# Adaptive-norm attention and gated feed-forward: the loop's products on tiles of 64 rows and 32 columns

## Chip, cores and metric

One core of a Trainium2 chip runs the whole program. The metric is the device time of one execution in microseconds (us). A program's engines are called PE (TensorE), DVE (VectorE), ACT (ScalarE), POOL (GpSimd) and SP (SyncE, which issues the DMAs); PEld is PE's weight load.

## The reference, cut to what matters

The input x has 2048 rows of 512. There are 32 query heads of 16, which share one key and one value head, and a feed-forward of 1792.

```
mod = silu(c) @ w_mod                      # six rows: sa, ca, ga, sb, cb, gb
h = layernorm(x) * (1 + ca) + sa
q, k, v = h @ wq, h @ wk, h @ wv           # q: 32 heads of 16; k, v: one head of 16
p = softmax(q k^T / 4)                     # 32 x 2048 x 2048
x = x + ga * ((p @ v) @ wo)
h = layernorm(x) * (1 + cb) + sb
x = x + gb * ((sigmoid(h @ w_gate) * (h @ w_up)) @ w_down)
```

## The kernel before, in words

A prologue normalises x, transposes it, and makes keys, values and the first q products. Then comes a loop of 512 steps: 32 units (4 blocks of 512 query rows, 8 units of four heads in each) with 16 steps, one for each 128 keys. A tail finishes the last block. Products other than the values are in 2-byte numbers, split into high and low halves and added up as three products; P, V and the transposes are 4-byte.

One step (the body from line 928) does the following on PE, in this order, which the code writes out and `Ordered` (line 110) pins:

- `scores(n)` four times (line 938): `st_tile` (495) multiplies 64 rows of keys and queries into a bank `st` of 128 keys by 512 queries, which ACT turns into P by an exponential; `a_tile` (443) multiplies queries and keys of a later unit (19 steps ahead) into a bank `sa`, of which DVE takes the row maximum `mx`. Both work on one half of the array's rows, and always on opposite halves, so the two run side by side. There are two `st` banks and two `sa` banks.
- `values()` twice with work in it (line 948): `pv` (509) multiplies P of two steps ago with V into the banks `c` and `c1`. One call is eight 4-byte matmuls on tiles of 64 rows and 32 columns, two row halves by four heads, with 256 queries each. In the trace each of them appears as two matmuls: a burst is 16, two passes of eight.
- `piece()` four times (line 908): a piece of what else PE has to do for an earlier block. These products come as a `Couple` (143) of two groups, one on each row half with its own bank: output projection `po`, gate and up projections `pgu`, down projection `pd`. One n of a couple is one such pair of 64-row products. There are two banks for them, so a couple starts when both banks of the last have been read by ACT and DVE (or ACT alone).
- in the first block `light` (915) instead: one or two pairs of q products a step, 24 in 17 steps.

The loop's feed-forward work begins with the second block. `plan` (885) takes a couple of 24 or more pairs, gives it n steps by `RATE` (4.5 pairs a step), and `places` (862) says how many pairs go into each of the steps' four places: the first half of the pairs is dealt over 2n - 1 places, then two places stay empty, and the second half is dealt over 2n - 1 more. `lead` keeps count of what runs ahead.

Unit 0 differs: its `st` bank is made by four products of 128 queries, and its values come as 16 matmuls of 128 queries a call. The first 76 `sa` products are issued ahead of the loop. In unit 31 there are none left.

Of the kernel before, what the change touches and what calls it, by code (L numbers as in the profile page):

```python
# [16 lines left out]
P = 128  # L17
# [33 lines left out]
RATE = 4.5  # L51
# [15 lines left out]
def adaln_mqa_glu_kernel(  # L67
# [35 lines left out]
    def sbank(name):  # L103
        return psum["s"].tile([P, 512], F32, tag=name, name=name, bufs=SBANKS[name]) if "s" in psum else bank(name)
# [5 lines left out]
    class Ordered:  # L110
        def __init__(self, engine):
            self.engine = engine
# [5 lines left out]
    pinned = []  # L118
    pe, dve, act = Ordered(nc.tensor), Ordered(nc.vector), Ordered(nc.scalar)

    class Group:
        def __init__(self, stage, n, name, term, end, begin=None):
            self.stage, self.n, self.name, self.term, self.end, self.begin = stage, n, name, term, end, begin
# [16 lines left out]
    class Couple:  # L143
# [3 lines left out]
        def part(self, n0, n1):  # L147
            if n0 == 0:
                for g in self.gs:
                    g.open()  # L150
            m = self.n // 2
            for n in range(n0, n1):
                for j in range(2):
                    g = self.gs[j ^ (n >= m)]
                    l_, r_ = g.term(n % m, slice(64 * j, 64 * j + 64))
                    pe.matmul(g.bank, l_, r_, start=(n == 0), stop=(n == self.n - 1))
            if n1 == self.n:
                for k, g in enumerate(self.gs):
                    g.end(g.bank, k == 1)
# [162 lines left out]
    kp = cp.tile([P, S], F16, name="kp")  # L322
# [111 lines left out]
    def get_q(i):  # L434
        b, u = units[i]
        o = u // 2
        if (b, o) not in qps:
            assert (b, o) in qdone
            load_q(b, o)
        return qps[b, o], 2 * (u % 2)  # L440


    def a_tile(i, n):
        qp, pr0 = get_q(i)
        if i not in mxs:
            mxs[i] = wp.tile([P, 4, 4, 4], F32, tag="mx", name="mx", bufs=2)
        h = n % 4
        kc, qt = (n // 4 % 4, n // 16) if i == 0 else (n // 16, n // 4 % 4)
        j, pr = heads[h]
        sa = sbank("sa")  # L450
        pe.matmul(sa, qp[64 * j:64 * j + 64, pr0 + pr, qt * P:(qt + 1) * P],  # L451
                  kp[64 * j:64 * j + 64, kc * 512:(kc + 1) * 512], start=True, stop=True)
        dve.tensor_reduce(mxs[i][:, 2 * j + pr, qt, kc:kc + 1], sa, axis=AX.X, op=ALU.max)  # L453
        if i == 0 and n % 16 == 15:
            pend.append((i, n // 16, n // 16 + 1))
        elif i > 0 and n == 63:
            pend.append((i, 0, 4))
# [32 lines left out]
    def parts(i, t):  # L490
        if i == 0:
            return [(4 * (t % 4) + n, slice(n * P, (n + 1) * P), slice(t // 4 * P, (t // 4 + 1) * P)) for n in range(4)]
        return [(t, slice(0, QB), slice(0, QB))]

    def st_tile(i, t, pr, j):
        qp, pr0 = get_q(i)
        if j == 0:
            P_["p"] = P2.tile([P, 2, 512], F32, tag=f"P{pr}", name=f"P{pr}", bufs=PBUFS)
        p_ = P_["p"]
        s_ = sbank("st")  # L500
        for kb, cols, qs in parts(i, t):
            pe.matmul(s_[:, cols], kp[64 * j:64 * j + 64, kb * P:(kb + 1) * P],
                      qp[64 * j:64 * j + 64, pr0 + pr, qs], start=True, stop=True)
        act.activation(p_[:, j], s_, AF.Exp, scale=0.25)
        Ps[i, t, 2 * pr + j] = p_[:, j]

# [133 lines left out]
    class Transposes:  # L640
        stage, n = "tr", 4
# [215 lines left out]
    run = []  # L857
    lead = [0.0]
# [1 line left out]


    def places(m, n):
        k = 2 * n - 1
        half = [m * (z + 1) // k - m * z // k for z in range(k)]
        return half + [0, 0] + half

    def pick(s):
        while main and main[0][0] is None:
# [16 lines left out]
    def plan(s):  # L885
        if s < NU * NKB:
            return
        if not run:
            g = pick(s)
            if g is None:  # L890
                lead[0] = 0.0
                return
            if g.stage == "tr":
                n, sizes = 1, [0, 4, 0, 0]
            else:
                least = -(-g.n // MOST)
                n = min(max(least, round((g.n + lead[0]) / RATE)), len(units) * NKB - s)
                if n < least:
                    spare.insert(0, g)
                    return  # L900
                sizes = places(g.n // 2, n)
            at = 0
            for z in sizes:
                run.append((g, at, at + z))
                at += z
        lead[0] += sum(z[2] - z[1] for z in run[:4]) - RATE

    def piece():
        if run:
            g, n0, n1 = run.pop(0)  # L910
            if n1 > n0:
                g.part(n0, n1)
# [10 lines left out]
    for i, (b, u) in enumerate(units):  # L923
# [4 lines left out]
        for kb in range(NKB):  # L928
# [9 lines left out]
            def scores(n):  # L938
                st_tile(i, kb, n // 2, n % 2)
                if an + (n ^ 1) < len(alist):  # L940
                    a_tile(*alist[an + (n ^ 1)])
# [10 lines left out]
                        pv(*z)  # L952

            scores(0)
            piece()
            values()
            scores(1)
            if b == 0:
# [2 lines left out]
            scores(2)  # L961
            for z in rows:
                z()
            piece()
            values()
            scores(3)
            piece()
# [65 lines left out]
```

## Time and profile before

| what | us |
|---|---|
| median of 3 runs (lowest to highest) | 1969.54 (1966.88 to 1969.86) |
| the profiled execution | 1967.33 |
| its span in the trace | 1965.5 |
| PE busy | 1865.7 |
| DVE busy | 1471.8 |
| ACT busy | 1242.5 |
| POOL busy | 642.3 |

The profile's page gives for each engine its busy time and number of instructions; for groups of equal instructions the count, the busy time together, the mean of one in ns, and the idle time of the engine ahead of them with what ended it. In the trace a matmul's record starts when its data start to move and ends by a model, about 0.16 us after the next one may start; so PE is read by the distance of starts, not by busy time. `64*128` in a row is the tile of the array that is used (64 rows, 128 columns), `64x512` the moving operand. A view in order of time merges equal neighbours: start, length from the first start to the last end, and the count. A view of stretches gives each engine's busy time and count within it, the clock granted to PE, and DMA.

### The profile page before, as it was taken

To read this page: it belongs to the slowest core of one execution; us is meant where nothing else is said; L and a number is where in the kernel's file an instruction comes from. 1 tells how busy PE (TensorE), PEld (TensorE's weight loads), DVE (VectorE), ACT (ScalarE), POOL (GpSimd) and SP (SyncE) were. 2 spreads that over 40 slices of the span, in tenths; PEclk is the share of its full clock that TensorE was granted. 3 is DMA by queue.
4 is the path that set the end of the run, shared out by engine and by line. 5 is a ranking of instruction groups with operands and counts; after the bars stand their busy time and mean duration, and the time that the engine had idled before them with its cause. 6 is when DMAs were issued, how large, how long until landed. Compare 5 with 4: busy or idle time off the path is not lost.

```text
span 1965.5 us, 58671 instructions
## 1 busy us (share of the span) xinstructions
PE 1865.7 (95%) x25787; PEld 630.8 (32%) x25787; DVE 1471.8 (75%) x2407; ACT 1242.5 (63%) x2263; POOL 642.3 (33%) x744
## 2 busy tenths in 40 slices
PE   6889999999999999999999999999999999998998
PEld 3344222222223333333323333333323333322444
DVE  8889999999887777777787777777788777741411
ACT  3258778888676666666676666666667666665100
POOL 4213444454353231322254131323144132122333
PEclk9679999999999999999999999999999999998999
DMA  6102222321001110101001010111010010011211
GB/s 239 57 13 81 67 90 89 102 62 55 22 18 40 34 40 5 46 32 33 31 26 40 27 51 5 35 32 42 22 37 30 26 51 16 16 33 42 74 65 54
DMA packets 66328, 92.41 MB, mean 47 GB/s; under 512 B 14752, under 2 KB 41376, under 8 KB 66072
## 3 DMA queue, kind: packets, MB, share of 16 engines
q1 hardware_dynamic: 66072, 88.66, 14.0%
q8 instruction: 202, 3.31, 0.7%
q14 instruction: 54, 0.44, 0.1%
HBM read 67.68 MB, written 16.22 MB: 43 GB/s over the span
## 4 chain that ended last, share of the span: by engine, by line
PE 82%; DVE 6%; ACT 5%; issue 2%; DMA 2%; POOL 1%; SPq 1%; POOLq 0%; ACTq 0%; DVEq 0%
PE c L116 28%; PE st L116 19%; PE pgu L116 10%; PE sa L116 9%; PE pd L116 4%; PE pgu L139 4%; DVE mx L116 3%; PE pd L139 2%; ACT P L116 2%; PE pq L116 2%; PE po L116 1%; ACT th L116 1%; PE sa L451 1%; DVE mx L453 1%; SPq L551 1%
## 5 line engine op out<-in xcount | busy, mean ns | idle before, releaser
L116 DVE TENSOR_REDUCE mx<-sa 128x1 f32<-128x512 f32 x1972 | 1269.3, 685 | 291.3 <-PE sa L116 287.5
L116 ACT ACTIVATE P<-st 128x512 f32<-128x512 f32 x2048 | 1137.0, 595 | 494.3 <-PE sa L116 443.2
L116 PE MATMUL st<-qp,kp 64*128 64x512 f16 (+1 forms) x2240 | 748.6, 364 | 15.0 <-ACT P L116 10.6
L116 PE MATMUL sa<-kp,qp 64*128 64x512 f16 x1972 | 730.6, 381 | 7.5 <-DVE mx L116 6.8
L116 PE MATMUL c<-P,V 64*32 64x256 f32 (+1 forms) x16896 | 680.1, 382 | 0.0
L116 PEld LDWEIGHTS c<-P,V 64*32 64x32 f32 x16896 | 193.5, 105 | 425.4 <-issue 407.4
L116 PEld LDWEIGHTS <-kp 64*128 64x128 f16 x2240 | 183.3, 94 | 441.5 <-issue 424.3
L116 PE MATMUL pgu<-h2h,gw 64*128 64x512 f16 x1312 | 258.2, 377 | 26.2 <-ACT th L116 18.0
L116 PEld LDWEIGHTS <-qp 64*128 64x128 f16 x1972 | 175.5, 93 | 108.0 <-issue 32.1
L116 PE MATMUL pgu<-h2l,gw 64*128 64x512 f16 x656 | 134.9, 378 | 0.0
L116 PEld LDWEIGHTS <-gw 64*128 64x128 f16 x1968 | 100.8, 94 | 105.2 <-issue 37.0
L732 POOL TENSOR_SCALAR th<-th 128x512 f32<-128x512 f32 x41 | 25.4, 619 | 313.2 <-ACT th L116 313.0
L542 POOL TENSOR_TENSOR cs<-cs,cs 128x512 f32<-128x512 f32 x31 | 39.3, 1268 | 181.6 <-DVE cs L116 169.3
L478 POOL TENSOR_SCALAR mh<-m 16x128 f16<-16x128 f32 (+1 forms) x34 | 9.8, 289 | 264.5 <-ACT m L116 264.5
L424 POOL MEMSET qp<- 32x2048 f16 x32 | 57.6, 1799 | 55.6 <-PE sa L116 49.3
L139 PE MATMUL pgu<-h2h,gw 128*128 128x512 f16 x240 | 71.9, 379 | 0.0
L738 POOL TENSOR_TENSOR gl<-th,gh 128x512 f16<-128x512 f32 x56 | 64.8, 1158 | 4.7
L116 PE MATMUL pd<-wdh,gh 64*128 64x512 f16 x280 | 56.4, 376 | 4.9 <-ACT ot L116 2.6
L726 ACT ACTIVATE th<-pgu 128x512 f32<-128x512 f32 x15 | 9.0, 597 | 80.6 <-PE pgu L139 80.6
L735 DVE SCALAR_TENSOR_TENSOR th<-th,pgu 128x512 f32<-128x512 f32 x15 | 10.3, 685 | 65.6 <-PE pgu L139 53.3
L737 POOL TENSOR_SCALAR gh<-th 128x512 f16<-128x512 f32 x56 | 34.8, 621 | 69.1 <-DVE th L735 65.5
L116 DVE COPY u<-pgu 128x512 f32<-128x512 f32 x41 | 27.9, 680 | 37.1 <-PE pgu L116 37.0
(167 smaller groups left out, 1435.9 us busy)
## 6 DMA issues: line engine op xcount, KB each, us to landing
gw<-wD SPq DMA_DIRECT2D x56, 512.0 KB
wD<-gw SPq DMA_DIRECT2D x14, 512.0 KB
wm<-in_w_mod_dram SPq DMA_DIRECT2D x6, 1024.0 KB
qp<-qD SPq DMA_DIRECT2D x96, 64.0 KB
xall<-in_A_x_dram SPq DMA_DIRECT2D x4, 1024.0 KB
qD<-q SPq DMA_DIRECT2D x16, 256.0 KB
raw<-cs SPq DMA_DIRECT2D x128, 32.0 KB
xr<-in_A_x_dram SPq DMA_DIRECT2D x16, 256.0 KB
```

The lines of the kernel that those rows point to most:

```text
L116: return (lambda *a, **k: keep(f_(*a, **k))) if pinned else f_
L139: pe.matmul(self.bank, l_, r_, start=(n == 0), stop=(n == self.n - 1))
L424: pool.memset(qp[j:j + 32], 0.0)
L451: pe.matmul(sa, qp[64 * j:64 * j + 64, pr0 + pr, qt * P:(qt + 1) * P], kp[64 * j:64 * j + 64, kc * 512:(kc + 1) * 512], start=True, stop=True)
L453: dve.tensor_reduce(mxs[i][:, 2 * j + pr, qt, kc:kc + 1], sa, axis=AX.X, op=ALU.max)
L478: pool.tensor_scalar(mh[:, 0], m32, 1.0, 0.0, op0=ALU.mult, op1=ALU.add)
L542: pool.tensor_tensor(cs, cs, cs1, op=ALU.add)
L551: sp.dma_start(dst[DH * g:DH * (g + 1)], cs[32 * hh + r0:32 * hh + r0 + DH])
L732: pool.tensor_scalar(th, th, 1.0, 1.0, op0=ALU.add, op1=ALU.mult)
L735: dve.scalar_tensor_tensor(th, th, 1.0, p_, op0=ALU.add, op1=ALU.mult)
L737: pool.tensor_scalar(hi, th, 1.0, 0.0, op0=ALU.mult, op1=ALU.add)
L738: pool.tensor_tensor(lo, th, hi, op=ALU.subtract)
```

## The change

A helper splits a product into four over the columns of the array. It is used for the scores `st`, for `sa` inside the loop, and for the pairs of couples; the q products of `light` are couples too. Products ahead of the loop and in the tail keep their 128 columns. The values had 64x32 tiles already.

The second part is where pieces stand. `piece()` is called at two places of a step instead of four: after the second scores and after the fourth. `places` deals the first half of a couple's pairs over n - 1 places and the second half over n, with one empty place between, so that a place holds two or three pairs.

```diff
+    def columns(dst, l_, r_, start, stop):
+        for c_ in range(0, P, 32):
+            pe.matmul(dst[c_:c_ + 32], l_[:, c_:c_ + 32], r_, start=start, stop=stop)
...
-                    pe.matmul(g.bank, l_, r_, start=(n == 0), stop=(n == self.n - 1))
+                    columns(g.bank, l_, r_, n == 0, n == self.n - 1)
...
-        pe.matmul(sa, qp[64 * j:64 * j + 64, pr0 + pr, qt * P:(qt + 1) * P],
-                  kp[64 * j:64 * j + 64, kc * 512:(kc + 1) * 512], start=True, stop=True)
+        l_, r_ = qp[64 * j:64 * j + 64, pr0 + pr, qt * P:(qt + 1) * P], kp[64 * j:64 * j + 64, kc * 512:(kc + 1) * 512]
+        if pinned:
+            columns(sa, l_, r_, True, True)
+        else:
+            pe.matmul(sa, l_, r_, start=True, stop=True)
...
-            pe.matmul(s_[:, cols], kp[64 * j:64 * j + 64, kb * P:(kb + 1) * P],
-                      qp[64 * j:64 * j + 64, pr0 + pr, qs], start=True, stop=True)
+            columns(s_[:, cols], kp[64 * j:64 * j + 64, kb * P:(kb + 1) * P],
+                    qp[64 * j:64 * j + 64, pr0 + pr, qs], True, True)
...
-        k = 2 * n - 1
-        half = [m * (z + 1) // k - m * z // k for z in range(k)]
-        return half + [0, 0] + half
+        k = [n - 1, n]
+        first, second = ([m * (z + 1) // q_ - m * z // q_ for z in range(q_)] for q_ in k)
+        return first + [0] + second
...
-                n, sizes = 1, [0, 4, 0, 0]
+                n, sizes = 1, [4, 0]
...
-        lead[0] += sum(z[2] - z[1] for z in run[:4]) - RATE
+        lead[0] += sum(z[2] - z[1] for z in run[:2]) - RATE
...
             scores(0)
-            piece()
             values()
             scores(1)
...
             for z in rows:
                 z()
-            piece()
             values()
             scores(3)
             piece()
```

On PE, around a burst of values in the middle of the loop (a step of the third block), there stood these rows: the last score product of one place (`sa`, weights from the queries `qp`), the burst on the banks `c` and `c1`, and the first score product of the next place (`st`, weights from the keys `kp`).

```order
L116 LDWEIGHTS qp
L116 MATMUL sa<-kp,qp 128x512
L116 MATMUL c<-P_14015,V 32x256 x2
L116 MATMUL c<-P_14042,V 32x256 x2
L116 MATMUL c_14158<-P_14015,V 32x256 x2
L116 MATMUL c_14158<-P_14042,V 32x256 x2
L116 LDWEIGHTS kp
L116 MATMUL st<-qp,kp 128x512
```

Now the same place reads as follows; of `sa` the last of four column products is shown, of `st` the first of four.

```order
L116 LDWEIGHTS qp
L116 MATMUL sa<-kp,qp 32x512
L116 MATMUL c<-P_23979,V 32x256 x2
L116 MATMUL c<-P_24036,V 32x256 x2
L116 MATMUL c_24160<-P_23979,V 32x256 x2
L116 MATMUL c_24160<-P_24036,V 32x256 x2
L116 LDWEIGHTS kp
L116 MATMUL st<-qp,kp 32x512
```

The order is the same; every output ahead of the burst and behind it now has the burst's 32 columns.

Between the bursts stood the pieces, on PE in the same stretch of the loop: one pair of gate or up products (`pgu`, weights from `gw`) after each pair of scores.

```order
L116 LDWEIGHTS gw
L116 MATMUL pgu<-h2h,gw 128x512
L116 LDWEIGHTS gw
L116 MATMUL pgu<-h2h,gw 128x512
L116 LDWEIGHTS kp
L116 MATMUL st<-qp,kp 128x512
L116 LDWEIGHTS qp
L116 MATMUL sa<-kp,qp 128x512
L116 LDWEIGHTS gw
L116 MATMUL pgu<-h2h,gw 128x512
```

Now a place holds two or three pairs, each of eight column products, and no score stands between them; shown is the border of two pairs.

```order
L116 LDWEIGHTS gw
L116 MATMUL pgu<-h2h,gw 32x512
L116 LDWEIGHTS gw
L116 MATMUL pgu<-h2l,gw 32x512
L116 LDWEIGHTS gw
```

Scores that stood between two pairs have moved ahead of them or behind them. The order of the instructions on ACT is the same as before, and on DVE but for one small instruction of the prologue; on POOL and SP a few neighbours changed places.

## Prediction

> **What bounds the kernel now.** I read the profile from the outside in. First the page: busy time by engine, and the chain that ended last.
>
> ```profile
> PE 1865.7 (95%) x25787; PEld 630.8 (32%) x25787; DVE 1471.8 (75%) x2407; ACT 1242.5 (63%) x2263; POOL 642.3 (33%) x744
> ...
> PE 82%; DVE 6%; ACT 5%; issue 2%; DMA 2%; POOL 1%; SPq 1%; POOLq 0%; ACTq 0%; DVEq 0%
> ```
>
> PE carries 82% of the chain. But a busy PE is not a full PE, so the question is what it does in a step. The stretches by stage come next; I cut them at the starts of units (64 exponentials each): unit 0, units 1 to 7, units 8 and 9, units 10 to 30, unit 31, tail.
>
> ```profile
> core 0: us, PE busy (x) PEld busy (x) DVE busy (x) ACT busy (x) POOL busy (x), PEclk, DMA share, GB/s
> 115.30:163.50 48.20, 46.85 (x1279) 29.47 (x1282) 40.69 (x65) 36.95 (x68) 6.04 (x11) 0.89 0.04 15
> 163.50:484.00 320.50, 313.67 (x4859) 95.18 (x4841) 292.81 (x473) 256.99 (x471) 147.72 (x179) 1.00 0.25 81
> 484.00:587.50 103.50, 98.30 (x1418) 29.72 (x1402) 87.56 (x144) 75.61 (x139) 44.45 (x60) 1.00 0.09 27
> 587.50:1756.30 1168.80, 1127.02 (x16340) 358.36 (x16336) 913.91 (x1454) 788.81 (x1447) 345.38 (x382) 1.00 0.10 31
> 1756.30:1812.80 56.50, 48.21 (x705) 13.66 (x709) 5.96 (x5) 36.17 (x68) 12.30 (x13) 0.91 0.13 39
> ```
>
> A unit takes 320.5/7 = 45.8 us where only q products run beside the attention, and 1168.8/21 = 55.7 us with feed-forward products: 3.48 us a step. 60% of the run lies in those 21 units, where no engine but PE is near full. So look at PE inside a step there.
>
> ```profile
> 1001.15 0.38 PE L116 MATMUL po<-woh,al 64*128 64x512 f16 x2
> 1001.37 0.38 PE L116 MATMUL po<-woh,ah 64*128 64x512 f16 x2
> ...
> 1002.32 0.66 PE L116 MATMUL c<-P,V 64*32 64x256 f32 x16
> 1002.92 0.39 PE L116 MATMUL st<-qp,kp 64*128 64x512 f16 x1
> ```
>
> A product on both row halves (x2) starts 0.22 us after the one before. A burst of values (x16: two passes of eight matmuls on 64x32 tiles) holds PE 0.60 us. What a pass costs when it has company of its own kind is seen at the loop's end, where 64 such matmuls stand in a row:
>
> ```profile
> 1812.42 0.39 PE L116 MATMUL st<-qp,kp 64*128 64x512 f16 x1
> 1812.73 1.48 PEld L116 LDWEIGHTS c<-P,V 64*32 64x32 f32 x64 [0.23 <-issue]
> 1812.73 1.96 PE L116 MATMUL c<-P,V 64*32 64x256 f32 x64
> ...
> 1814.62 0.11 PEld L139 LDWEIGHTS <-ah 128*128 128x128 f16 x2 [0.41 <-issue]
> ```
>
> From 1812.73 to 1814.62 are 1.89 us for eight passes. Less the 0.60 of a lone burst of two, six more passes take 1.29 us: **0.215 us a pass**, with eight tiles side by side, as long as a product pair. So a lone burst pays 0.60 - 0.43 = 0.17 us for leaving the shape. Entering costs too: st at 1812.42 gives way after 0.31 us, 0.10 more than a product. Together 0.27 us; the chain of waits says the same:
>
> ```profile
> 1002.17 0.22 PE po L116 x2
> 1002.39 0.59 PE c L116 x16
> 1002.98 0.32 PE st L116
> ```
>
> 0.59 + 0.32 - 2 x 0.215 - 0.215 = 0.265 us of empty array per burst; two bursts a step, 16 steps a unit: **8.5 us a unit**.
>
> **The change part by part.** The same work is issued as 64x32 tiles, so the loop's matmuls have one shape and the two bursts of a step change it no longer. A product pair becomes eight matmuls on eight tiles; I price it at the 0.215 us of the pass above, since the moving bytes are equal: 256 columns of 4 bytes there, 512 of 2 here.
>
> Units 10 to 30, PE. The rows of the stretch 587.5 to 1756.3, grouped by line:
>
> ```profile
> L116 PE MATMUL pgu<-h2h,gw 64*128 64x512 f16 x1218 | 236.1, 376 | 18.9 <-ACT th L116 17.2 <-ACT ot L116 1.6
> L116 PE MATMUL pgu<-h2l,gw 64*128 64x512 f16 x610 | 122.8, 376 | 0.0
> L116 PE MATMUL pd<-wdh,gh 64*128 64x512 f16 x280 | 56.4, 376 | 4.9 <-ACT ot L116 2.6 <-ACT th L116 2.2
> ...
> L116 PE MATMUL po<-woh,ah 64*128 64x512 f16 x64 | 13.7, 375 | 1.8 <-ACT ot L116 1.3 <-ACT t L116 0.5
> ```
>
> With three times 280 pd and three times 64 po these are 2860 matmuls, 1430 pairs, 4.25 a step. A step then holds 4 pairs of scores, 4.25 feed-forward pairs and 4 passes: 12.25 x 0.215 = 2.63 us, **42.1 us a unit**. Today's 55.7 is this, 8.5 of shape changes, and 5.1 of waits and broken pairs. When the 8.5 go, what is late next is DVE. Its work in the same stretch:
>
> ```profile
> L116 DVE TENSOR_REDUCE mx<-sa 128x1 f32<-128x512 f32 x1333 | 863.7, 685 | 241.8 <-PE sa L116 240.6
> L116 DVE COPY u<-pgu 128x512 f32<-128x512 f32 x38 | 25.9, 680 | 2.7 <-PE pgu L116 2.5
> L116 DVE COPY cs<-c 128x512 f32<-128x512 f32 x21 | 14.5, 690 | 2.3 <-PE c L116 1.4
> ```
>
> Their pace without waits is seen ahead of the loop, in the order of time on DVE:
>
> ```profile
> 73.64 5.46 DVE L453 TENSOR_REDUCE mx<-sa 128x1 f32<-128x512 f32 x9
> ```
>
> Nine maxima in 5.46 us are (5.46 - 0.685)/8 = 0.597 us apart, though one lasts 0.685. DVE's floor is 1333/21 x 0.597 = 37.9 us a unit, and (913.91 - 863.7)/21 = 2.4 us for the other 121 instructions of the stretch: 40.3. That is 1.8 below PE's floor, and the 241.8 us that DVE waits for sa today is the room it has. Are two sa banks enough? A bank's round:
>
> ```profile
> 300.82 1.88 DVE L116 TENSOR_REDUCE mx<-sa 128x1 f32<-128x512 f32 x3
> ...
> 302.46 0.39 PE L116 MATMUL sa<-kp,qp 64*128 64x512 f16 x1
> ...
> 302.75 0.37 PE L116 MATMUL sa<-kp,qp 64*128 64x512 f16 x1
> ...
> 302.91 0.69 DVE L116 TENSOR_REDUCE mx<-sa 128x1 f32<-128x512 f32 x1 [0.21 <-PE sa L116]
> ```
>
> Product start to maximum 0.45 (302.46 to 302.91), the maximum 0.69, and 0.05 until the next product in the bank (300.82 + 1.88 = 302.70, then 302.75): 1.19 us, 0.595 per sa. The new places (nothing between the first two scores but one burst, then two or three pairs, then one burst) put sa every 0.645 or 0.645 to 0.86 us, so any two in a row take 1.29 us or more: the plain step waits for no bank. DVE's 2.4 us of other work eat that margin (0.1 per two sa), and I let PE pay two thirds of them: 1.6 us a unit at least. The upper end is today's 5.1. I take 4.4, near the present, as every wait still breaks a pair: 46.5 us a unit, 9.2 less, times 21 = **193 us**. The evacuations that a next group waits for (18.9 and 4.9 us idle ahead of pgu and pd in the rows) get a burst and two pairs of scores of cover where they had one pair; that is inside the 4.4.
>
> Units 1 to 7. PE: 24 q pairs in 17 steps, (4 + 1.41 + 4) x 0.215 x 16 = 32.4 us, 40.9 with today's shape changes. DVE: 38.2 of maxima and at most 2.1 for the 473/7 - 64 = 3.6 others, 40.3. Today's 45.8 is the two disturbing each other. Afterwards DVE alone bounds it, at 0.60 per sa by the bank's round (0.02 more as the fourth column starts last): 40.5 us, and I take 41.5. 4.3 x 7 = **30 us**.
>
> Units 8 and 9 have feed-forward products for part of the time: 17 us of shape changes go, DVE's 144 operations at 0.6 allow no more than 103.5 - 86; I take **12**. Unit 31 has no sa: its 8.5 go, **8**. Unit 0 has products of 128 columns, four to a tile, which become sixteen: I take **0** (from -8.5 to +10, below). Prologue and tail keep their shapes; ACT issues its instructions in the same order, DVE all but one, POOL and SP but for a few neighbours: 0.
>
> Sum: 193 + 30 + 12 + 8 = 243. The profiled execution took 1967.3 us (span 1965.5): 1724. The median of the runs is 2.2 above it, and I add 2 for the column starts: **1728**.
>
> **What before cannot show: issue.** Units 10 to 30 now issue 785 PE instructions each, 49 a step; counted in the new order it is 2366, 148 a step. Nothing in this trace issues that many for long. Nearest from below, weight load and matmul of 16 columns in turn:
>
> ```profile
> 67.36 0.17 PE L373 MATMUL pv<-wkvh,h1l 128*128 128x16 f16 x1
> ...
> 68.26 0.17 PE L373 MATMUL pv<-wkvh,h1l 128*128 128x16 f16 x1
> ```
>
> These are the first and last of 37 matmuls: 0.90 us for 36 steps, 12.5 ns an instruction. From above, unit 0 sustains 1168 instructions in 48.2 us, 41 ns each, but it waits for DVE, so it bounds little. At 12.5 a feed-forward unit needs 29.6 us of issue and hides under 42.1; it decides from 55.7/2366 = 23.5 ns on. I take the lower row, being a stream of this kind, and keep both ends.
>
> [...]
>
> **The rivals.** *Issue bounds the loop (slower).* At 28 ns an instruction, between the two rows, 2366 take 66 us a unit (+10.6 x 21 = 222), the 1626 of a unit before them 45.5 (0), unit 0's 3316 take 93 (+45), units 8, 9 and 31 about 5: 2240 us. For it: triple the count, and no row near it for long. Against: 12.5 ns where it was tried. At 22 ns a unit takes 52.1 and unit 0 73: 77 + 30 + 12 + 8 - 25 = 102 are left, 1865.
>
> *The eight half-precision tiles do not hide their loads (slower).* Loads grow fourfold; at the c load's 0.105 us exposed once per pair, 21 x 16 x 8.25 x 0.105 = 291 us are added to 1728: 2020.
>
> ```profile
> L116 PEld LDWEIGHTS c<-P,V 64*32 64x32 f32 x16896 | 193.5, 105 | 425.4 <-issue 407.4
> L116 PEld LDWEIGHTS <-kp 64*128 64x128 f16 x2240 | 183.3, 94 | 441.5 <-issue 424.3
> ```
>
> Against it: the 64 loads at 1812.73 all end inside their matmuls. [...] The rows show 105 ns against 94, no more.
>
> *The two sa banks (smaller gain).* If waits stay at 5.1 and DVE's 2.4 are lost in full, a unit is 49.6 and units 1 to 7 gain nothing: 1967 - 128 - 20 + 4 = 1823. For it: both engines then stand within 2 us of each other, with two banks between them. Against: the even places.
>
> *The change does little:* the array may empty around a burst because c is 4-byte and the rest 2-byte, not for the shape. Then 0.27 a burst stays and only the places count: within a few us of 1967. Against it, a type change without a change of shape:
>
> ```profile
> 44.98 0.38 PE L139 MATMUL pq<-h1l,wdh 128*128 128x512 f16 x1
> 45.19 0.93 PE L339 MATMUL pt<-ident,xall 128*128 128x128 f32 x7
> 45.95 0.38 PE L139 MATMUL pq<-h1h,wdl 128*128 128x512 f16 x1
> ```
>
> The 4-byte pt starts 0.21 us after the 2-byte pq, a product's own time, and pq follows seven pt after 0.76, 0.109 each: nothing is lost.
>
> **How the numbers follow.** Forecast case, 1690 to 1800: 0.69. Banks or slower issue, 1800 to 1960: 0.13. The change does little: 0.02. Issue or loads beyond the point of decision: 0.16. The low end 1690 has feed-forward waits of 2.6 (38 less); the high end 1850 takes in the banks and issue up to nearly 22 ns. Faster by over 0.2% (about what a measurement of this kernel can tell): 0.82; slower 0.16.
>
> **What would show it.** In the profile after: the chain's c rows at 0.43 with no 0.32 behind; pairs of st and sa as eight starts in 0.05 us, 0.215 from group to group; units 10 to 30 near 46.5 us and units 1 to 7 near 41.5; DVE's idle before mx down from 241.8 to between 50 and 130 there. PE gaps that end in "issue", groups of eight spread wider than 0.215, and a unit 0 well above 48 would prove the issue rival; loads of kp, qp or gw that end before their matmuls start, the load rival. A granted clock below 1.00 in the loop would spoil all of it: it is 1.00 today.

## The result, and the profile after

The changed kernel takes **1796.32 us** (median of 4 runs, 1792.44 to 1800.48) against 1968.55 us beside it on the same chip: ratio 0.9126, 95% interval 0.9098 to 0.9154. It is faster, by 172 us; the forecast was 1728, 68 us lower. The profiled execution took 1799.62 us. The page of the profile after, in its order (engines, DMA queues, chain, two groups):

```profile
span 1797.8 us, 105503 instructions
...
PE 1677.6 (93%) x48719; PEld 1067.2 (59%) x48719; DVE 1479.2 (82%) x2407; ACT 1281.8 (71%) x2263; POOL 643.0 (36%) x744
...
q8 instruction: 381, 6.24, 1.5%
...
PE 70%; DVE 16%; ACT 5%; issue 4%; POOL 3%; DMA 2%; SPq 1%; POOLq 0%; ACTq 0%; DVEq 0%
...
L116 DVE TENSOR_REDUCE mx<-sa 128x1 f32<-128x512 f32 x1972 | 1276.5, 686 | 123.8 <-PE sa L116 61.9
...
L116 PE MATMUL c<-P,V 64*32 64x256 f32 (+1 forms) x16896 | 755.4, 373 | 12.4 <-issue 11.9
```

PE's instructions have nearly doubled (2 x 48719 records against 2 x 25787), and time that the chain can only call "issue" has gone from 2% to 4%. VectorE's share of the chain has risen more, from 6% to 16%; what that is worth, e5 shows. One row got no attention in the prediction: queue 8 carries instructions. Its 381 packets of 6.24 MB / 381 = 16.4 KB are 2 x 48719 / 381 = 255.7 PE instructions each; on the page of before the row had 202 packets, 2 x 25787 / 202 = 255.3. **A packet is 256 PE instructions here.**

By stage, cut as before (unit 0, units 1 to 7, 8 and 9, 10 to 30, 31):

```profile
core 0: us, PE busy (x) PEld busy (x) DVE busy (x) ACT busy (x) POOL busy (x), PEclk, DMA share, GB/s
117.20:185.10 67.90, 48.40 (x2356) 36.99 (x2342) 41.53 (x65) 37.72 (x69) 4.92 (x10) 0.92 0.04 12
185.10:487.90 302.80, 286.49 (x8426) 171.07 (x8414) 290.31 (x473) 259.74 (x470) 147.48 (x179) 1.00 0.27 87
487.90:586.40 98.50, 90.06 (x2570) 53.52 (x2554) 87.76 (x145) 76.80 (x140) 45.16 (x60) 0.97 0.10 30
586.40:1599.00 1012.60, 980.59 (x32945) 674.51 (x32930) 922.71 (x1453) 823.19 (x1446) 345.77 (x382) 1.00 0.13 38
1599.00:1645.70 46.70, 38.52 (x1255) 25.08 (x1247) 5.96 (x5) 36.46 (x67) 12.09 (x13) 0.93 0.16 49
```

| stage | before | after | gain | forecast gain |
|---|---|---|---|---|
| start and tail | 268.0 | 269.3 | -1.3 | 0 |
| unit 0 | 48.2 | 67.9 | -19.7 | 0 |
| units 1 to 7 | 320.5 | 302.8 | 17.7 | 30 |
| units 8 and 9 | 103.5 | 98.5 | 5.0 | 12 |
| units 10 to 30 | 1168.8 | 1012.6 | 156.2 (48.2 a unit) | 193 (46.5) |
| unit 31 | 56.5 | 46.7 | 9.8 | 8 |

The forecast sum was 243 us, and the spans differ by 168. Three quarters of the 75 us between them stand in two places: unit 0 got slower by 20 us, and the long stretch gained 37 us less than forecast. Units 1 to 9 gained 19 us less.

The mechanism that was to bring the gain did. The chain in a plain stretch of a feed-forward unit:

```profile
1002.62 0.43 PE pgu L116 x16
1003.05 0.17 PE sa L116 x4
1003.22 0.05 PE st L116 x4
1003.27 0.43 PE c L116 x16
1003.70 0.17 PE st L116 x4
1003.87 0.05 PE sa L116 x4
```

A burst of values holds the array 0.43 us in place of 0.59, and the scores behind it 0.17 + 0.05 in place of 0.32: no time is lost at the change between products and values. A group of eight follows the last after 0.215 us here, so the loads, four times as many, are hidden.

What is new is seen best in unit 0. The chain there, and PE in order of time:

```profile
141.76 1.40 issue
...
145.61 1.01 issue
...
148.96 1.76 issue
```

```profile
148.34 0.62 PE L116 MATMUL c<-P,V 64*32 64x128 f32 x23
150.72 0.42 PE L116 MATMUL c<-P,V 64*32 64x128 f32 x9 [1.76 <-issue]
```

PE stops in the middle of a burst, of which 23 matmuls have run, for 1.76 us. Such stops of 0.9 to 1.8 us come every 3.2 to 4.3 us. Counting the instructions between one stop and the next (the three stretches lie between neighbouring stops):

```profile
139.40:141.72 2.32, 2.29 (x128) 1.88 (x128) 1.54 (x3) 1.58 (x3) 0.00 (x0) 1.00 0.03 7
143.10:145.60 2.50, 2.44 (x128) 1.89 (x128) 1.35 (x3) 1.49 (x3) 0.00 (x0) 1.00 0.02 7
146.60:148.97 2.37, 2.34 (x127) 1.77 (x128) 1.42 (x3) 1.39 (x3) 0.00 (x0) 1.00 0.02 7
```

128 matmuls and 128 loads: one packet of 256 (255 once). PE uses a packet up in 2.3 to 2.5 us and then stands. That it stands for the next packet shows in when it goes on. Take as a stop every distance of over 0.4 us between the starts of two neighbouring instructions of PE (matmuls and loads). Unit 0 has 16 from 120 us on, and 15 of them end 1.1 to 1.7 us after a packet of queue 8 has landed; chance would put 16% there (0.6 us of the 3.70 that a packet takes). The bounds of 1.1 and 1.7 us are read from this unit; the other stages and runs are a test of them.

In the feed-forward units the matter is less plain. What ended waits there (us in total, number, longest), and the packets:

```profile
PEld L116 <- issue: 111.4, 287, 3.8
...
DVE mx L116 <- PE st L116: 34.2, 85, 1.1
DVE mx L116 <- PE sa L116: 28.1, 74, 1.6
...
PE st L116 <- ACT P L116: 10.8, 31, 0.6
...
PE sa L116 <- DVE mx L116: 10.0, 21, 3.3
```

```profile
q8 instruction: 257, 4.21, 1.8%
```

The loads' waits on "issue" can't be taken for waits on packets: in the same stretch of before there were more of them, at half the packets.

```profile
PEld L116 <- issue: 342.7, 799, 1.8
```

```profile
q8 instruction: 127, 2.08, 0.7%
```

The ends of the stops say more: here 34 of 117, 29%, end 1.1 to 1.7 us after a packet landed, where chance would put 15% there. So the supply of instructions takes part, but not alone; PE's matmuls also wait for VectorE or ScalarE, 21 us in all, and its loads 10 us for VectorE. A unit issues (32945 + 32930) / 21 = 3137 instructions, 12.25 packets, and uses one per 1012.6 / 257 = 3.94 us. At the rate of the plain stretch, sixteen instructions (eight loads, eight matmuls) per 0.215 us, a packet would take 3.44 us and the unit 42.1; at unit 0's 3.70 us a packet the unit would take 45.3, and it takes 48.2. Before, a packet was used in 9.2 us.

**Theory S (supply):** PE's instructions reach it at no more than 256 per 3.5 to 3.9 us, and where the split raises their number, that sets the time. **Theory B (banks):** the units are held by the round of VectorE and the two `sa` banks, and "issue" is only how the remaining unevenness shows. For unit 0 the rival is anything but its number of instructions.

### The profile page after: what moved, and what is told of

The parts are those of the page before. It is cut to its first block, busy times and chain, and to the rows that moved or that the text cites. A ratio compares the mean times of both kernels' runs of the same rounds, so it can differ in the third digit from the quotient of the medians.

```text
span 1797.8 us, 105503 instructions
## 1 busy us (share of the span) xinstructions
PE 1677.6 (93%) x48719; PEld 1067.2 (59%) x48719; DVE 1479.2 (82%) x2407; ACT 1281.8 (71%) x2263; POOL 643.0 (36%) x744
## 3 DMA queue, kind: packets, MB, share of 16 engines
q8 instruction: 381, 6.24, 1.5%
## 4 chain that ended last, share of the span: by engine, by line
PE 70%; DVE 16%; ACT 5%; issue 4%; POOL 3%; DMA 2%; SPq 1%; POOLq 0%; ACTq 0%; DVEq 0%
PE c L116 19%; PE st L116 12%; DVE mx L116 12%; PE pgu L116 11%; PE sa L116 10%; PE pd L116 4%; PE pgu L143 4%; ACT P L116 4%; PE pd L143 3%; PE pq L116 1%; PE po L116 1%; PE sa L459 1%; DVE mx L460 1%; PE pmod L226 1%; ACT cs L116 1%
## 5 line engine op out<-in xcount | busy, mean ns | idle before, releaser
L116 PE MATMUL st<-qp,kp 64*32 64x512 f16 (+1 forms) x8960 | 838.0, 362 | 40.2 <-ACT P L116 22.7
L116 PE MATMUL sa<-kp,qp 64*32 64x512 f16 x7888 | 811.0, 381 | 17.2 <-DVE mx L116 11.5
L116 PE MATMUL c<-P,V 64*32 64x256 f32 (+1 forms) x16896 | 755.4, 373 | 12.4 <-issue 11.9
L116 PEld LDWEIGHTS <-kp 64*32 64x32 f16 x8960 | 312.3, 92 | 232.6 <-issue 135.9
L116 PEld LDWEIGHTS c<-P,V 64*32 64x32 f32 x16896 | 354.6, 106 | 84.9 <-issue 25.9
L116 PEld LDWEIGHTS <-qp 64*32 64x32 f16 x7888 | 326.0, 90 | 127.9 <-issue 64.6
L116 PE MATMUL pgu<-h2h,gw 64*32 64x512 f16 x5248 | 284.9, 378 | 9.0 <-DVE u L116 5.7
L116 PEld LDWEIGHTS <-gw 64*32 64x32 f16 x7872 | 155.3, 92 | 66.4 <-issue 25.6
L116 PE MATMUL pgu<-h2l,gw 64*32 64x512 f16 x2624 | 161.7, 378 | 0.2 <-issue 0.2
L116 PE MATMUL pd<-wdl,gh 64*32 64x512 f16 x1120 | 70.6, 376 | 0.0
L733 ACT ACTIVATE th<-pgu 128x512 f32<-128x512 f32 x15 | 9.0, 597 | 77.6 <-PE pgu L143 73.3
```

Of the source, the lines that this page charges most:

```text
L116: return (lambda *a, **k: keep(f_(*a, **k))) if pinned else f_
L733: act.activation(th, p_, AF.Tanh, scale=0.5 / (SH * SW))
```

## The experiments

All edits are shown against the changed kernel. This table has what the runs gave; a packet's time is the length of units 10 to 30 over the packets of queue 8 in them, so it follows from the unit's time and explains nothing by itself.

| run | ratio to before (95%) | unit 0 | units 1-7 | a unit of 10-30 | its PE instructions | us a packet |
|---|---|---|---|---|---|---|
| before | 1 | 48.2 | 320.5 | 55.7 | 1556 | 9.20 |
| changed kernel | 0.9126 (0.9098-0.9154) | 67.9 | 302.8 | 48.2 | 3137 | 3.94 |
| e1 unit 0's `st` whole | 0.9331 (0.9316-0.9345) | 102.1 | 303.3 | 48.3 | 3137 | 3.95 |
| e2 columns, four places | 0.9337 (0.9311-0.9364) | 71.0 | 303.9 | 49.9 | 3138 | 4.08 |
| e3 two places, no columns | 0.9721 (0.9706-0.9737) | 48.2 | 320.5 | 53.2 | 1557 | 8.73 |
| e4 tiny copies | 1.0019 (0.9999-1.0038) | 68.5 | 318.8 | 55.0 | 3649 | 3.86 |
| e5 half the maximum | one run, 1777.03 us | 67.5 | 290.7 | 47.9 | 3137 | 3.92 |
| e6 64 columns | 0.9852 (0.9836-0.9869) | 51.9 | 327.0 | 53.8 | 2083 | 6.61 |
| e8 unit 0 as before | 0.9075 (0.9054-0.9096) | 48.0 | 300.6 | 48.5 | 3137 | 3.96 |
| e9 values once, two places | 0.9540 (0.9526-0.9555) | 51.6 | 331.4 | 51.0 | 2625 | 4.98 |
| e10 values once, three places | 0.9161 (0.9146-0.9176) | 48.2 | 299.3 | 49.2 | 2625 | 4.81 |
| e11 half maximum, half values | one run, 1765.64 us | 68.3 | 290.1 | 47.4 | 3136 | 3.87 |
| e12 values in 2 bytes | 0.8583 (0.8564-0.8603) | 42.8 | 293.6 | 45.0 | 2624 | 4.39 |
| e13 the same, unit 0 split | one run, 1700.69 us | 53.6 | 292.4 | 45.0 | 2625 | 4.40 |

And this one has PE's stops of over 0.4 us in units 10 to 30, and how many of them end 1.1 to 1.7 us after a packet has landed. Chance is 0.6 us over the time of a packet; where the share is at chance, the supply does not show.

| run | stops | ending so | share | share by chance | length of those, us |
|---|---|---|---|---|---|
| before | 102 | 8 | 8% | 7% | 5.6 |
| changed kernel | 117 | 34 | 29% | 15% | 22.8 |
| e4 tiny copies | 228 | 183 | 80% | 16% | 138.3 |
| e5 half the maximum | 134 | 56 | 42% | 15% | 38.3 |
| e10 values once, three places | 121 | 16 | 13% | 13% | 10.0 |
| e11 half maximum, half values | 272 | 152 | 56% | 15% | 115.3 |
| e12 values in 2 bytes | 164 | 25 | 15% | 14% | 15.0 |

### The two halves of the change: e2 and e3

e2 keeps the four places of before and only splits the columns; e3 keeps only the new places.

For e2 (and `piece()` again at four places):

```diff
-        k = [n - 1, n]
-        first, second = ([m * (z + 1) // q_ - m * z // q_ for z in range(q_)] for q_ in k)
-        return first + [0] + second
+        k = 2 * n - 1
+        half = [m * (z + 1) // k - m * z // k for z in range(k)]
+        return half + [0, 0] + half
```

For e3 (and the same for `sa` and the couples):

```diff
-            columns(s_[:, cols], kp[64 * j:64 * j + 64, kb * P:(kb + 1) * P],
-                    qp[64 * j:64 * j + 64, pr0 + pr, qs], True, True)
+            pe.matmul(s_[:, cols], kp[64 * j:64 * j + 64, kb * P:(kb + 1) * P],
+                      qp[64 * j:64 * j + 64, pr0 + pr, qs], start=True, stop=True)
```

> The split alone: all products of the loop on 64x32 tiles, pieces in the old four places. Theory S: as many instructions as the changed kernel, so the supply bounds it equally; the places only give the next couple's banks less cover (18.9 and 4.9 us of PE idle before) and put sa unevenly, +0.5 to +1.5 us a feed-forward unit: 1806 to 1830. Theory B (what is short of the forecast is lost between DVE and PE over the two sa banks): uneven sa cost more, +3 us a unit: 1860 or more. If the places were the gain: near 1968.

> The two places alone, products on 64x128 tiles as before. Both theories: the two shape changes a step stay (0.27 us each), so the gain is at most the broken pairs: 1945 to 1975, that is within 1.2% of before. If the places were most of the gain: below 1880.

Split alone: 1836.79 us, a gain of 132, 7 us beyond the slow end of what S expected. Places alone: 1911.2, a gain of 57, well beyond what was expected of them; 2.4 us a feed-forward unit. So the split brings most of the gain. 132 + 57 = 189 is more than the 172 of both: e3's 53.2 less the 8.5 of shape changes would be 44.7, but with the columns the unit stops at 48.2. Something new holds it there. In both e2 and the changed kernel unit 0 is long, in e3 it is not.

### More instructions for next to no work: e4

In units 1 to 31 each `st` is followed by a copy of its first eight query columns, which `st`'s bank gets a second time. That is 512 instructions a unit.

```diff
+            if i > 0:
+                columns(s_[:, 0:8], kp[64 * j:64 * j + 64, kb * P:(kb + 1) * P],
+                        qp[64 * j:64 * j + 64, pr0 + pr, 0:8], True, True)
```

> The changed kernel; each st product of units 1 to 31 is followed by a copy of its first 8 query columns (the same values are written again): 32 PE instructions more a step, almost no work for the array. Theory S: 512 instructions more a unit are two blocks of 3.5 us: units 10 to 30 go from 48.2 to about 55 us (+150 in all), units 1 to 7, which need only 2394/256 x 3.5 = 33 of their 43 us, stay within 1.5 us: total 1930 to 1960. Theory B with enough supply: only the array time of the copies counts, four tiles at once and 0.025 us or so a group, 0.1 us a step, the same in all units: +1.6 x 31 = 50, total about 1845.

1969.62 us, 10 above the upper end of what S expected: the whole gain is gone. Units 10 to 30:

```profile
602.50:1757.70 1155.20, 1055.81 (x38320) 700.49 (x38305) 937.25 (x1453) 828.43 (x1447) 345.63 (x382) 1.00 0.11 34
```

(38320 + 38305) / 21 = 3649 instructions are 14.25 packets; at the changed kernel's 3.94 us each these would last 56.1 us, and the unit takes 55.0. The added 6.8 us for 512 instructions are 13.3 ns each. The array's part in them is small: a pair of scores gives way to the next product after 0.241 us in the median, in place of 0.216, which makes 64 x 0.025 = 1.6 us a unit. And 80% of PE's stops now end 1.1 to 1.7 us after a packet landed. What hardly burdens the array, 8 columns in place of 512, burdens the loop by its count. Units 1 to 7, which were to stay within 1.5 us, went from 302.8 to 318.8 us, at 2918 instructions a unit.

### Less work for the same instructions: e5 and e11

e5 takes VectorE's maximum over half of its columns. e11 also gives the array less: a values matmul of 128 columns in place of 256, in 14 of 16 steps. The first two places of the diff are e5, all three are e11; the scale only keeps the numbers finite.

```diff
-        dve.tensor_reduce(mxs[i][:, 2 * j + pr, qt, kc:kc + 1], sa, axis=AX.X, op=ALU.max)
+        dve.tensor_reduce(mxs[i][:, 2 * j + pr, qt, kc:kc + 1], sa[:, 0:256] if pinned else sa, axis=AX.X, op=ALU.max)
...
-        act.activation(p_[:, j], s_, AF.Exp, scale=0.25)
+        act.activation(p_[:, j], s_, AF.Exp, scale=0.01)
...
+            if 0 < t < NKB - 1:
+                cut = slice(cut.start + QB // 4 * (t % 2), cut.start + QB // 4 * (t % 2 + 1))
```

> The changed kernel with the loop's row maximum read from 256 of the 512 columns only (half of it is left out) and the exponential's scale at 0.01, so that every number stays finite: VectorE loses about half of the time of its largest group, TensorE's work and its instructions stay as they are. Theory S (TensorE's instructions arrive at about 3.9 us per 256, and 3134 of them set a feed-forward unit): units 10-30 stay at 47 to 48.2 us each, the whole at 1780 to 1797. Theory B (the round of VectorE and its bank that each row score waits for): the units fall to 43 to 44, the whole to 1690 to 1710.

> The changed kernel with VectorE's maximum over 256 of 512 columns, the exponential's scale at 0.01 so that the numbers stay finite, and in 14 of 16 steps of a unit each values matmul over 128 of its 256 columns (both halves are left out): VectorE's floor falls to about 27 us a feed-forward unit and the array's from 42.1 to about 36, while TensorE's 3134 instructions a unit stay. Theory S: 44 to 48 us a unit in units 10-30. If array, VectorE and their waits set the pace: 42 or less.

Units 10 to 30 of e5, then of e11, and VectorE's waits there in e11:

```profile
568.90:1575.50 1006.60, 969.16 (x32949) 612.98 (x32934) 612.95 (x1453) 825.45 (x1447) 345.99 (x382) 1.00 0.13 39
```

```profile
568.70:1564.10 995.40, 897.18 (x32936) 569.98 (x32922) 614.59 (x1453) 792.42 (x1446) 346.29 (x382) 0.99 0.13 39
```

```profile
DVE mx L116 <- PE sa L116: 221.0, 515, 2.0
DVE mx L116 <- PE st L116: 104.0, 209, 1.9
```

VectorE's busy time falls from 922.7 to 613 us, PE's from 981 to 897, and VectorE now waits 325 us for PE. The unit goes from 48.2 to 47.9 and 47.4, where array, VectorE and their waits would have let it fall to 42. (The whole of e5 took 1777.03 us, 3 below the lower end of S.) The time that the engines save turns into stops of PE: 42% and 56% of these end 1.1 to 1.7 us after a packet landed, in place of 29%. Theory B falls here for the changed kernel: at this number of instructions lighter engines hardly shorten a unit. The 0.3 us of e5 are no more than equal units differ by from run to run (48.2, 48.3 in e1, 48.5 in e8); both together bring 0.8. So the changed kernel stands just above a floor that is largely the supply's. In units 1 to 7 half the maximum gives 12 us (41.5 a unit in place of 43.3): there, at 2406 instructions a unit, VectorE still sets the pace in part.

### Unit 0: e8, e1 and e13

e8 leaves unit 0 as it was:

```diff
+        w_ = P if now[0] < NKB else 32
-        for c_ in range(0, P, 32):
-            pe.matmul(dst[c_:c_ + 32], l_[:, c_:c_ + 32], r_, start=start, stop=stop)
+        for c_ in range(0, P, w_):
+            pe.matmul(dst[c_:c_ + w_], l_[:, c_:c_ + w_], r_, start=start, stop=stop)
```

e1 leaves only unit 0's `st` whole (`whole` is one matmul of 128 columns):

```diff
-            columns(s_[:, cols], kp[64 * j:64 * j + 64, kb * P:(kb + 1) * P],
-                    qp[64 * j:64 * j + 64, pr0 + pr, qs], True, True)
+            (columns if i > 0 else whole)(s_[:, cols], kp[64 * j:64 * j + 64, kb * P:(kb + 1) * P],
+                                          qp[64 * j:64 * j + 64, pr0 + pr, qs], True, True)
```

> The changed kernel with the products of unit 0 whole, as they were, and those of units 1 to 31 split. Theory S: unit 0 issues about 2940 instructions in place of 4700 and goes from 67.8 us back to 48; every other stage as in the changed kernel, so 1775 to 1780. If unit 0 is slow for another reason (the new places, or a low clock), it stays above 60 and the whole at 1790 or more.

> The changed kernel, with the st products of unit 0 whole again (128 columns) and everything else split. Theory S (PE's instructions arrive in blocks of 256, no faster than one block in about 3.5 us, a 4-byte matmul counting as four instructions): unit 0 has 1536 instructions less, so 3160/256 = 12.3 blocks x 3.64 = 45 us instead of 67.9; the shape changes in it come back, and it takes 46 to 51 us. Total about 1778 (1796 less 18). Rival W (the narrow products of unit 0 are slow on the array itself, not their supply): the total would be the same, but 1 to 2 us gaps ending in nothing would still be seen in unit 0, at the same distance of about 3.6 us. Rival N (unit 0 was lengthened by something else, such as the granted clock of 0.92 there): unit 0 stays near 68, total 1796.

e8 has its unit 0 back at 48.0 us, and takes 1785.96 us, 6 above the upper end expected, as units 10 to 30 came out 6 us longer than in the changed kernel. So unit 0's 20 us come from its split products; the new places stand in e8 too. e1 missed by 57 us. Its unit 0 (the column behind POOL is the granted clock):

```profile
118.50:220.60 102.10, 101.60 (x1587) 53.91 (x1589) 44.17 (x65) 39.24 (x68) 6.04 (x11) 0.51 0.02 7
```

The clock granted to PE is 0.51 over the whole unit, where it is 0.92 in the changed kernel and 0.89 in e8, and PE is busy all the time. So the run says nothing on the instructions of unit 0; its other stages are those of the changed kernel. Why the clock stayed low with whole `st` among split `sa`, q products and values was not settled.

e13 is the changed kernel with P and V in 2 bytes (its edit follows), and asks the question of unit 0 again, with a smaller count and all of it split.

> The changed kernel, unit 0 split, with P and V in 2 bytes. Unit 0 issues 1024 instructions fewer, about 3670 in place of 4700. Theory S: 14.4 blocks at 3.64 us, 52 us for unit 0 in place of 67.8; from unit 1 on as the kernel with P and V in 2 bytes and unit 0 whole. If unit 0 is slow for another reason than its instructions: 64 or more.

```profile
115.20:168.80 53.60, 40.13 (x1880) 28.07 (x1864) 40.77 (x65) 37.20 (x69) 4.91 (x10) 0.89 0.04 14
```

The changed kernel's 2356 + 2342 = 4698 instructions are 18.35 packets in 67.9 us, 3.70 us each. At that rate e13's 1880 + 1864 = 3744, 14.6 packets, would last 54.1 us; they took 53.6. The array's work is smaller too in e13, but PE was busy for only 48.40 of the changed kernel's 67.90 us. In e13 11 of 20 stops end behind a packet, so other waits have a part there as well.

### Wider tiles: e6

```diff
-        for c_ in range(0, P, 32):
-            pe.matmul(dst[c_:c_ + 32], l_[:, c_:c_ + 32], r_, start=start, stop=stop)
+        for c_ in range(0, P, 64):
+            pe.matmul(dst[c_:c_ + 64], l_[:, c_:c_ + 64], r_, start=start, stop=stop)
```

> The changed kernel with tiles of 64 rows and 64 columns in place of 32, the values still at 32. A feed-forward unit issues about 2080 instructions in place of 3134 (8.1 blocks of 256, 32 us at 3.9 us each), so the supply does not set it; unit 0 issues about 3525, 51 us. If any change of tile size drains the array (0.27 us per change, as in the kernel before), units 10-30 go back to those of the two places alone, 53 us each, and the whole to 1905 to 1920. If only the step from 128 columns to fewer drains, there is neither drain nor shortage: 45 to 46.5 us each and 1715 to 1740.

1938.99 us, 19 above the upper end; the units 53.8, near e3's 53.2. Units 1 to 7 took 327.0 us, 6.5 more than before, which was not expected and is not explained. The chain around a burst:

```profile
1001.73 0.59 PE c L116 x16
1002.33 0.33 PE st L116 x2
```

0.59 and 0.33, where the kernel before has 0.59 and 0.32. A change of the tile's width from 64 to 32 costs here as much as one from 128 to 32: 0.59 + 0.33 - 3 x 0.215 = 0.275 us a burst, against 0.265. So the split must go down to the 32 columns of the values, and its price in instructions can't be halved that way.

### Fewer instructions: e9, e10, e12

e9 and e10, both with unit 0 as in e8, issue the values as eight matmuls of 512 columns once a step in place of twice eight of 256, which saves 512 instructions a unit at equal work of the array. e9 does so from unit 1 on and puts both feed-forward places behind the third scores; e10 does so from unit 8 on and deals the feed-forward over three places.

```diff
-            cut = slice(half * QB // 2, (half + 1) * QB // 2)
-            ps = [(t, cut, cut)]
+            ps = [(t, slice(0, QB), slice(0, QB))] if half == 1 else []
...
             scores(0)
             values()
+            if i > 0:
+                values()
             scores(1)
-            if b == 0:
-                light(s)
-            piece()
             scores(2)
             for z in rows:
                 z()
-            values()
+            if b == 0:
+                light(s)
+            piece()
+            piece()
+            if i == 0:
+                values()
             scores(3)
-            piece()
             values()
```

In e10 the step reads so from unit 8 on, with the feed-forward dealt over 3n - 2 places in place of 2n - 1:

```diff
             scores(0)
             values()
+            if b > 0:
+                values()
             scores(1)
             if b == 0:
                 light(s)
             piece()
             scores(2)
             for z in rows:
                 z()
-            values()
+            if b == 0:
+                values()
+            else:
+                piece()
             scores(3)
             piece()
```

> The kernel with unit 0 whole, and for units 1 to 31 the values as one burst of 8 matmuls of 512 columns after the first scores of a step in place of two bursts of 8 by 256, and the step's two places for the feed-forward next to each other after the third scores. The array's work is the same; a feed-forward unit issues 512 instructions fewer, about 2620 (10.2 blocks, 40 us at 3.9 us), less than the array's own 42.1 us. Theory S: units 10-30 at 44 to 46.5 us each, the whole at 1700 to 1745. Theory B: the uneven spacing lengthens the row scores' waits, units at 48 or more and the whole at 1775 or more.

> The kernel with unit 0 whole, and in units 8 to 31 the values as one burst of 8 matmuls of 512 columns after a step's first scores, with the feed-forward of a step in three places, one after each of the other scores, so that no two scores follow each other directly. Units 1 to 7 keep the changed kernel's order. A feed-forward unit issues about 2620 instructions in place of 3134 for the same work of the array. Theory S (supply at 3.9 us per 256): 40 us of supply, below the array's 42.1, so 43.5 to 46.5 us a unit in units 10-30 and 1690 to 1745 for the whole. Theory B (what sets the units is the spacing of the row scores and the wait for VectorE and its banks, in which case a burst of values of double length costs as much as in the kernel with the values once and two neighbouring places): 49 to 51 us a unit and 1800 to 1840.

Both missed S's numbers and came out as expected of B: 51.0 and 49.2 us a unit. So in this order the supply did not set them (in e10 13% of the stops end behind a packet, as by chance), and lifting it gained nothing. In e9 units 1 to 7, without feed-forward, went from 43 to 47 too. In e10 PE's longest named wait in units 10 to 30 is for a bank of `st`:

```profile
PE st L116 <- ACT P L116: 27.1, 60, 0.8
PE sa L116 <- DVE mx L116: 10.3, 25, 2.4
```

27.1 us against 10.8 in the changed kernel, but these are 1.3 us a unit and not all of the cost. Two bursts evenly spaced are worth more here than the instructions that they take: 48.5 us a unit in e8, which has them, against 51.0 and 49.2. That the longer burst sends the scores closer together than ScalarE and VectorE can follow is a guess, which no run shows; how it would come to 4 us a unit or more is left open.

e12 keeps order and spacing and takes the instructions away by the type: P and V in 2 bytes, with unit 0 as in e8. A 4-byte matmul is a load and a matmul twice over, a 2-byte one does it once: the values have 16896 loads and as many matmuls in e8, and 8448 in e12.

```diff
-    V = cp.tile([P, NKB, 32], F32, name="V")
+    V = cp.tile([P, NKB, 32], F16, name="V")
...
-            P_["p"] = P2.tile([P, 2, 512], F32, tag=f"P{pr}", name=f"P{pr}", bufs=PBUFS)
+            P_["p"] = P2.tile([P, 2, 512], F16, tag=f"P{pr}", name=f"P{pr}", bufs=PBUFS)
```

> The kernel with unit 0 whole, and the exponentials P and the values V in 2 bytes in place of 4, all else in the changed kernel's order and places. A values matmul then is two instructions in place of four: a feed-forward unit issues about 2620 in place of 3134, evenly spaced as before, and the array's work falls by about 7 us a unit as well; that less work of the array alone moves a unit by under 1 us was shown by the kernel with half the maximum and half the values (47.4 us). Theory S (supply at 3.87 us per 256): the supply needs 39.6 us, VectorE 40.3, so 41.5 to 45 us a unit in units 10-30 and 1660 to 1710 for the whole. If something else holds the units (the spacing, as the kernel with the values once in three places may say): 47 to 49 us and 1760 or more.

**1689.6 us**, 0.8583 of before (0.8564 to 0.8603), the fastest here:

```profile
545.90:1490.40 944.50, 890.68 (x27561) 527.81 (x27553) 888.86 (x1454) 778.70 (x1446) 344.85 (x382) 0.99 0.13 40
```

45.0 us a unit, at the upper end of what S expected. The array's work fell as well, but e11 has shown that this, even with half the maximum, brings 47.4 at 3136 instructions; as far as these two can be set side by side, the 2.4 us beyond it go with the count. The packet now takes 4.39 us, the stops end behind a packet no more often than by chance, and VectorE is busy for 889 of 945 us.

## Why the prediction was right, and where its sizes were off

- **Shape changes, 0.27 us a burst.** Right, in mechanism and size: 0.43 + 0.22 in place of 0.59 + 0.32, and e6 brings 0.59 and 0.33 back with 64 columns. That also refutes the rival of the type: c stayed 4-byte and the loss is gone.
- **Loads hidden.** Right. Loads of 90 to 106 ns end inside the matmuls before them; eight loads for every 0.215 us leave no gap between the groups.
- **The two banks.** The rival named a unit of 49.6, near the 48.2 that came, by a cause that isn't the one: PE's matmuls waited for `mx` 10.0 us and its loads 9.8 in all of units 10 to 30, and with half the maximum (e5) the unit moved by 0.3 us. VectorE's idle ahead of `mx` fell there to 77.6 us, inside the 50 to 130 of the prediction:

```profile
L116 DVE TENSOR_REDUCE mx<-sa 128x1 f32<-128x512 f32 x1332 | 871.3, 687 | 77.6 <-PE st L116 34.2 <-PE sa L116 28.1
```

- **"At 12.5 a feed-forward unit needs 29.6 us of issue and hides under 42.1."** This is the step that failed, twice. It counted 2366 instructions, where the chip issues 3137. A burst of values went in as eight instructions, its eight matmuls, but each 4-byte matmul is load, matmul, load, matmul, 32 in all (32 bursts x 24 more = 768). The prediction's own rows had it: (16340 + 16336) / 21 = 1556 records a unit before, where it counted 785, and 1279 + 1282 in unit 0, 18.8 ns each, where it counted 1168 at 41. With the right count 42.1 us hide no more than 13.4 ns an instruction, and it had no long stream that ran so fast. And it took 12.5 ns from a row of 37 matmuls with their loads, about 73 instructions: fewer than a packet, so the row could only show how fast PE uses what it has, not how fast more comes. The runs put the price at 13.3 ns for each instruction added (e4), 14.5 in unit 0 (67.9 us / 4698) and at most 15.4 in the changed kernel's units (48.2 / 3137), against the 13.4 that could be hidden. A feed-forward unit lost 1.8 us against the forecast, 37 us in all. At the same count e11 stays 0.9 above the forecast with far lighter engines, so about half of the loss can be laid to the supply; the other half went with the work of VectorE and the array, through waits whose shares were not told apart.
- **Unit 0 at 0, from -8.5 to +10.** Mis-sized by the same step: 19.7 us lost. Sixteen products in place of four for each `st` make 4698 instructions there, and PE stood 22.4 us in the 15 stops that end behind a packet. The prediction had counted 3316 and named a long unit 0, with gaps that end in "issue", as the mark of the issue rival. This is what came, in a mild form.
- **Units 1 to 7 at 41.5.** Measured 43.3. A lighter VectorE (e5, 41.5) brings it to the forecast, and so do values in 2 bytes (e12, 41.9), which spare the array and the count alike. The stops do not show the supply there: 12 of 71, 17%, end behind a packet, where chance gives 13%. So VectorE does not hold these units alone, as assumed; what else does was not settled.
- **The places.** The forecast gave them no term of their own, only waits of 4.4 in place of 5.1. Alone they are worth 2.4 us a unit (e3). With them, and had the split only taken away the shape changes, the forecast would have been too slow, not too fast: 53.2 - 8.5 = 44.7 against 46.5.
- **The issue rival.** Its two prices, 28 and 22 ns an instruction, were chosen between the rows of 12.5 and 41; no run shows either. The runs gave 13.3 to 15.4, and not as an even price: in unit 0 PE issues 256 instructions between two stops in 2.3 to 2.5 us, 9 to 10 ns each, and then stands for 0.9 to 1.8 us.

The mechanism of the gain was right, and its size in the array too. That the time lay just inside the forecast's own case (1690 to 1800) was in part luck: the case had issue hidden in the feed-forward units, and it was not. The shortfalls of 20, 37, 12 and 7 us happened to stop 4 us short of its end.

## What to carry to other kernels

Splitting matmuls over smaller tiles bought equal shapes (a burst and what follows it take 0.43 + 0.22 us in place of 0.59 + 0.32) and was paid for in instructions (3137 a unit in place of 1556). Count them as the chip issues them (each load, each matmul, a 4-byte matmul as four) and set count x 13 to 15 ns, the price of this kernel, against the stage's floor. The packets of the instruction queue on the profile's page, 256 PE instructions each, tell how near it is: here 9.2 us a packet was free, at 4.4 the supply did not show, and below 4 it did. Whether a stop is a wait for a packet is read from when it ends, not from the number of waits on "issue". A rate read from fewer than 256 instructions in a row is no evidence for a sustained one (here 12.5 ns from 73, against 13.3 to 15.4), and where the count binds, a type that needs one pass in place of two can pay twice: in e12 2624 instructions a unit in place of 3137, and PE busy for 891 us in place of 981 in units 10 to 30.

## What the runs showed of the hardware that was not expected

- Instructions come to PE in packets of 256 here, and in unit 0, where PE uses one up in 2.3 to 2.5 us, it stops about once a packet for 0.9 to 1.8 us. A packet's turn took 3.70 us in the changed kernel's unit 0, 3.66 in e13's and 3.87 in e2's (71.0 us for as many instructions), and 3.86 us in e4's feed-forward units. What makes the difference was not tried.
- Only part of a turn is the transfer. In the changed kernel's unit 0 a packet moved for 0.9 to 1.4 us; PE went on 1.1 to 1.7 us after it had landed, and the next packet began mostly 1.0 to 1.3 us after that. So the next one seems to be asked for only when PE goes on; this is read from the times, and was not tried.
- A step from 64 to 32 columns cost as much as one from 128 to 32: 0.59 + 0.33 us around a burst in e6, 0.59 + 0.32 before.
- With `st` on 128 columns, and `sa`, q products and values on 32, unit 0 ran at a granted clock of 0.51 for 102 us (e1). In e8, with `sa` and q products whole too, it was 0.89.
